# Five edits to an RWKV-then-soft-MoE kernel: queue of a small load, width and place of the v products, width of the second expert product, split of the last weight

## The chip, the cores and the metric

The kernel runs on one core of one Trainium2 chip. The metric is device time in microseconds, of the whole program. The kernel before takes 122.67 us, the median of 3 runs (122.54 to 122.88). The profile is one execution of the same program, with a span of 120.5 us (122.36 us by the metric).

## The reference

Two stages follow each other. The first is a linear attention with a decay for each channel (batch 4, 8 heads, 768 positions, head size 48); the second a soft mixture of experts (8 experts of 4 slots, model width 384, hidden width 1024) over all 3072 tokens.

```
for t in range(S):
    cur = einsum('bhd,bhe->bhde', u * k[t], v[t])
    y[t] = einsum('bhd,bhde->bhe', r[t], state + cur)
    state = w * state + einsum('bhd,bhe->bhde', k[t], v[t])
x = y as (B*S, H*D)
logits = x @ phi
d = softmax of logits over the tokens;   slot_input = d.T @ x
h = relu(slot_input[e] @ w1[e]);         slot_out[e] = h @ w2[e]
out = (softmax of logits over the slots) @ slot_out
```

## The kernel before, in words

**Units of work.** Two heads form a pair. A batch has 4 pairs, so there are 16 pairs, `nU`, numbered m or mu. A sequence of 768 is cut into 6 chunks of 128 positions, and these into two groups of three, `G = 2` and `L = 3`. A step i is one pair and one group: `mu, odd = divmod(i, 2)`, 32 steps in all, `nH`. The loop begins at i = -5, as the work is staged ahead: the step does the output of i, the state and mask of i + 1, and the preparation of the pair mu + 2.

**How the decay is taken in.** Instead of a loop over positions, k and r are scaled by powers of w: `W[0]` and `W[1]` are exp(position times ln w), built in the first steps by VectorE (line 188) and ScalarE (line 192). w itself comes to the core twice: `w_row`, one row which TensorE spreads over the partitions (`spread`, lines 177 and 178), and `wu`, from which `wu_steps` makes columns.

**The functions of a step.** `scale` multiplies raw k or r by W into kr (on GpSimd from the second pair on, line 228). `t_pe` transposes kr into the PSUM bank T0 (k, in even steps) or T1 (r, in odd steps), `t_evac` copies it to kT or rT on ScalarE (line 241). `b_pe` and `b_evac` turn kT back into kn, in order of position. `prod_f` multiplies kT by the transposed r. `v_cast` turns v to bf16 (line 270, ScalarE; GpSimd for the first pair). v lies in memory with three neighbouring positions in one partition; `v_pe` puts it in order of position with products by shifted parts of Q3 (line 284), into the bank Vb, and `v_evac` copies it to vn (line 290). `a_pe` multiplies kT by rT into Ab, `mask_f` masks it into AT (VectorE, line 304). `m_pe` builds the state of the chunks and the u term in Mb, `z_evac` makes Z and dv of it on VectorE (lines 341 and 342). `y_pe` adds up the output in Yb (lines 352, 363, 365), `y_evac` copies it to x (line 372, ScalarE).

**Routing.** From step 8 to step 31 `route` does the first part of the second stage for a batch that is done: transposes of x (`xt_mm`, then `xt_ev`, line 396, on ScalarE), logits, their exponential Le (line 402), the sums over tokens (`disp`, line 422) and the transposes of Le (`le_t`, `let_ev`). In `route`, s counts the eight steps of one batch; part 2 holds the ScalarE copies.

**Order.** Each instruction is recorded in the order in which the Python code calls it (`O(...)`), and each engine runs its own instructions in this order. The order of calls in a step, of those that the change touches or stands beside, is: `a_pe`, `mask_f`, `y_pe`, `y_evac`, `v_pe`, `v_evac`, `m_pe`, `z_evac`, `prod_f` or `b_pe`, `scale`, `route` part 0, `t_pe`, `route` part 1, `t_evac`, `v_cast`, `route` part 2, then exponentials of W and rows of zt where `T_AT` and `Z_AT` say so.

**Transfers.** SyncE issues k, r and v of the four batches in pieces (lines 115 and 119), each as soon as its place in three `raw` buffers is free. GpSimd issues the expert weights, w1 to w1_all and w2 into `raw` buffers that the batches have left (lines 135 and 138), at the steps in `W_AT`: the first at step 13, after a copy into `guard` that waits for the k of the last batch. The last weight, expert 7 of w2, is cut into three pieces along y.

**The end.** After the loop the experts run: a first product with w1 (line 623), its relu, transposes (line 648), and `second`, the product with w2 (line 660), which adds both groups of four experts into SO. Experts 6 and 7 come last, each as its weights land. SO is scaled into `so` in two halves, by VectorE (line 671) and ScalarE (line 672). Then 24 products of LexpT by so (line 684) are scaled and written out (lines 686, 688, 704).

The calls of a step that the change moves:

```
        if 0 <= i + 2 < nH:
            v_pe(i + 2)
            v_evac(i + 2)
...
        if odd == 0 and 0 <= mu + 2 < nU:
            v_cast(mu + 2)
        route(i, 2)
```

Of the kernel before, what the change touches and what calls it, by code (L numbers as in the profile page):

```python
# [9 lines left out]
def kernel(  # L10
# [13 lines left out]
    B, H, S, D = r.shape  # L24
    C = 128
    nC = S // C
    Nn, Dm = out.shape
    ES = moe_phi.shape[1]
    E = moe_w1.shape[0]
    F = moe_w1.shape[2]  # L30
    Spe = ES // E
    nM = Dm // C
    nF = F // C
    nQ = H // 2
    G = 2
    L = nC // G
    T = L * C
    P2 = 2 * D
    nN = Nn // C
    nG = B * G  # L40
    nU = B * nQ
    nH = nU * G
    J = S // C
    JV = T // C

    f32 = mybir.dt.float32
    bf = mybir.dt.bfloat16
    i32 = mybir.dt.int32
    AF = mybir.ActivationFunctionType
    ALU = mybir.AluOpType  # L50

    def O(ins):
        return tc.keep_in_program_order(ins)

    pe, dve, act, pool, sp = nc.tensor, nc.vector, nc.scalar, nc.gpsimd, nc.sync

    big = ctx.enter_context(tc.tile_pool(name="big", bufs=1))
    cst = ctx.enter_context(tc.tile_pool(name="cst", bufs=1))
    wk = ctx.enter_context(tc.tile_pool(name="wk", bufs=3))
# [5 lines left out]
    EG = E // 2  # L65
# [4 lines left out]
    def w2_of(e):  # L70
        g, j = divmod(e, EG)
        return raw[1 + g][:].bitcast(bf)[:, j * eW2:(j + 1) * eW2].rearrange("p (y d) -> p y d", y=nF)

    def raw_of(which, b):
        return raw[b % NR][:, which * RW:(which + 1) * RW]
# [5 lines left out]
    Yb = psb.tile([128, 512], f32, name="Yb")  # L81
    Xb = psb.tile([128, 512], f32, name="Xb")
    Vb = psb.tile([128, 512], f32, name="Vb")
# [11 lines left out]
    w_row = early[0:1, 0:H * D]  # L95
# [5 lines left out]
    phi_f = late[:, 128:128 + nM * ES]  # L101
    wu = cst.tile([8, 128], f32, name="wu")
    wu3 = wu[:].rearrange("q (e s) -> q e s", s=64)
    O(dve.memset(wu[:], 1.0))
    O(sp.dma_start(out=w_row, in_=w.rearrange("(o h) d -> o (h d)", o=1)))
    O(act.preload_act_table_set("natural_log_exp_and_others"))
    O(act.dma_start(out=wu3[0:4, :, 0:D], in_=w.rearrange("(q e) d -> q e d", e=2)))
    O(act.dma_start(out=wu3[4:8, :, 0:D], in_=u.rearrange("(q e) d -> q e d", e=2)))
# [44 lines left out]
    Q3 = cst.tile([128, QW], bf, name="Q3")  # L153
# [59 lines left out]
    ones = cst.tile([128, 128], bf, name="ones")  # L213
    Le_t = [cst.tile([128, L, 128], bf, name=f"Le{j}") for j in range(2)]
    phi_s = cst.tile([128, nM, ES], bf, name="phi_s")
    phi_b = cst.tile([128, nM * ES], bf, name="phi_b")
    assert JV == nM
    acc = cst.tile([128, NA], f32, name="acc")
    guard = cst.tile([128, 1], f32, name="guard")
    st = {}  # L220

# [51 lines left out]
    def at(i):  # L273
        m, g = divmod(i, G)
        b, q = divmod(m, nQ)
        return m, b, q, g, b * G + g

    def v_pe(i):
        m, b, q, g, n = at(i)
        vb = st["vb", m]  # L280
        for c in range(L):
            for j in range(JV):
                o = C * c - j + JV - 1
                O(pe.matmul(Vb[:, c * P2:(c + 1) * P2], Q3[:, o:o + C], vb[:, :, g, j, :],  # L284
                            start=(j == 0), stop=(j == JV - 1)))

    def v_evac(i):
        vn = wk.tile([128, L, 2, D], bf, name="vn", bufs=3)
        st["v", i] = vn
        O(act.copy(vn[:].rearrange("p c e d -> p (c e d)"), Vb[:, 0:L * P2]))  # L290

    def a_pe(i):
        m, b, q, g, n = at(i)
        kT, rT = st["kT", m], st["rT", m]
        for c in range(L):
            t = slice((g * L + c) * C, (g * L + c + 1) * C)
            for e in range(2):
                s = slice(64 * e, 64 * e + 64)
                O(pe.matmul(Ab[:, e, c * C:(c + 1) * C], kT[s, t], rT[s, t]))  # L299

    def mask_f(i):
        AT = wk.tile([128, 2, L, C], bf, name="AT", bufs=2)
        st["AT", i] = AT
        O(dve.tensor_mul(AT[:], Ab[:, :, 0:T].rearrange("p e (c t) -> p e c t", c=L),  # L304
                         mask_ut[:, None, None, :].to_broadcast([128, 2, L, C])))
# [99 lines left out]
    def le_t(n, lp=None):  # L405
        Le = st["Le", n]
        lp = le_p if lp is None else lp
        for c in range(L):
            O(pe.transpose(lp[:, c * C:(c + 1) * C], Le[:, c, :], ident[:]))
# [19 lines left out]
    def disp_ev(n, ds_p):  # L429
        if n == 0:  # L430
            O(dve.tensor_copy(acc[:], ds_p))
        else:
            O(dve.tensor_add(acc[:], acc[:], ds_p))
# [37 lines left out]
    Wf = [t[:].rearrange("p q j d -> p (q j d)") for t in W]  # L471
# [22 lines left out]
    for i in range(-5, nH):  # L494
        mu, odd = divmod(i, 2)
        if 0 <= i + 1 < nH:
            a_pe(i + 1)
            mask_f(i + 1)
        if pend:
            disp_ev(*pend.pop())  # L500
        if i == nH - 1:
            turn(n0, (2,), Vb[:].bitcast(bf), act)
            disp(n0 - 1, ds_t)
            le_t(n0 - 1)
            let_ev(n0 - 1, None, dve)
        if 0 <= i < nH:
            y_pe(i)
            y_evac(i)
        if 0 <= i + 2 < nH:
            v_pe(i + 2)  # L510
            v_evac(i + 2)
        if 0 <= i + 1 < nH:
            m_pe(i + 1)
            z_evac(i + 1)
        if odd == 0 and 0 <= mu + 1 < nU:
            prod_f(mu + 1)
        if odd and i > 0 and mu + 2 < nU:
            b_pe(mu + 2)
            b_evac(mu + 2)
        if odd and 0 <= mu + 3 < nU:  # L520
            scale(mu + 3, 0)
        if not odd and 0 <= mu + 2 < nU:
            scale(mu + 2, 1)
        route(i, 0)
        if 0 <= mu + 2 < nU:
            t_pe(mu + 2, odd)
            route(i, 1)
            t_evac(mu + 2, odd)
            if odd and i < 0:
                b_pe(mu + 2)  # L530
                b_evac(mu + 2)
        else:
            route(i, 1)
        if odd == 0 and 0 <= mu + 2 < nU:
            v_cast(mu + 2)
        route(i, 2)
        if i == nH - 3:
            turn(n0, (0, 1), T0, act)
        if i == nH - 2:
            turn(n1, (0, 1), T1, act)  # L540
        for f, j, q in T_AT.get(i, ()):
            f(j, q)
        if i in (-4, -3):
            wu_steps(i + 4)
        if i in Z_AT:
            q = Z_AT[i]
            O(act.activation(out=zt[:, q, 2, :], in_=zt[:, q, 0, :], func=AF.Copy, scale=wT[:, q:q + 1]))
        if i == 2:
            O(pool.memset(ones[:], 1.0))
            for t in Le_t:  # L550
                O(pool.memset(t[:], 0.0))
        if i == 3:
            load_kr(0, k, B - 1, 0, H)
            load_kr(1, r, B - 1, 0, H)
            for h0 in range(0, H, 2):
                load_v(B - 1, h0, h0 + 2)
        if i == 5:
            O(act.copy(phi_b[:], phi_f))
        if i == 6:
            for mi in range(nM):  # L560
                for j in range(nM):
                    o = C * mi - j + nM - 1
                    O(pe.matmul(Xb[:, mi * ES:(mi + 1) * ES].rearrange("p (j g s) -> p j g s", g=2, s=Spe),
                                Q3[:, o:o + C],
                                phi_b[:, j * ES:(j + 1) * ES].rearrange("p (g j s) -> p j g s", g=2, s=Spe),
                                start=(j == 0), stop=(j == nM - 1)))
            O(act.copy(phi_s[:].rearrange("p m s -> p (m s)"), Xb[:, 0:nM * ES]))
        if i == 28:
            O(pool.memset(uns, 0.0))
        if i == min(W_AT):  # L570
            O(pool.tensor_copy(guard[:], raw_of(0, B - 1)[:, 0:1]))
        for _ in range(W_AT.get(i, 0)):
            load_w(nw)
            nw += 1
    assert nw == 2 * E - 1
    for y0, y1 in ((0, 4), (4, 6), (6, 8)):
        load_w(nw, y0, y1)


# [29 lines left out]
    csr = cst.tile([128, 1], f32, name="csr")  # L609
# [8 lines left out]
    hT = [Wf[1].bitcast(bf)[:, g * F:(g + 1) * F].rearrange("p (y c) -> p y c", c=C) for g in range(2)]  # L618
    for g in range(2):
        for a in range(2):  # L620
            for mi in range(nM):
                for j in range(EG):
                    O(pe.matmul(hb[g][a][32 * j:32 * j + 32, 0:FH], uns[:, mi, g, j, :],
                                w1_all[:, g * EG + j, mi, a * FH:(a + 1) * FH],
                                start=(mi == 0), stop=(mi == nM - 1), skip_group_check=True))
            src = hb[g][a][:, 0:FH].rearrange("p (q y) -> p y q", y=nF)
            dst = h_sb[g][:, :, a * PH:(a + 1) * PH]
# [15 lines left out]
    HD = Dm // 2  # L643
# [7 lines left out]
        if g == 0:  # L651
            row_sums(0, 8)
    row_recip(0, 8)
    SO = [Xb[:, 0:HD], Yb[:, 0:HD]]

    def second(g, experts):
        for y in range(nF):
            for x in range(2):
                for j in experts:
                    O(pe.matmul(SO[x][32 * j:32 * j + 32, :], hT[g][:, y, 32 * j:32 * j + 32],  # L660
                                w2_of(g * EG + j)[:, y, x * HD:(x + 1) * HD],
                                start=(g == 0 and y == 0), stop=(g == 1 and y == nF - 1), skip_group_check=True))

    second(0, range(EG))
    second(1, range(EG - 2))
# [1 line left out]
    second(1, (EG - 2,))  # L667
    second(1, (EG - 1,))
    row_sums(8, 12)
    so = cst.tile([128, Dm], bf, name="so")  # L670
    O(dve.tensor_scalar_mul(so[:, 0:HD], SO[0], csr[:, 0:1]))
    O(act.activation(out=so[:, HD:Dm], in_=SO[1], func=AF.Copy, scale=csr[:, 0:1]))
    row_recip(8, 12)

    out_v = out.rearrange("(p n) m -> p n m", n=nN)
# [14 lines left out]
    i = 0  # L690
# [44 lines left out]
```

The softmax here doesn't subtract the row's maximum and nothing guards it: scores larger than these inputs give would overflow.

## Time and profile before

| what | value |
|---|---|
| time, median of 3 runs | 122.67 us (122.54 to 122.88) |
| span of the profile | 120.5 us, 4334 instructions |
| TensorE busy | 102.6 us, 85% |
| VectorE busy | 96.4 us, 80% |
| ScalarE busy | 83.7 us, 69% |
| GpSimd busy | 59.7 us, 50% |
| read from HBM, written | 39.38 MB, 4.72 MB |
| v products (line 284) | 288 of 128x96, 18.2 us busy |
| copies of v (line 290) | 32 of 128x288, mean 419 ns |
| casts of v (line 270) | 15 of 128x576, mean 677 ns |
| copies of kT, rT (line 241) | 32 of 128x768, mean 800 ns |

A busy time counts each instruction from its start to its end, and products overlap each other, so that 288 products of 211 ns take far less than their sum on the engine. How close they stand is read from the chain of waits or the timeline, which give when each group starts. A wait "A <- B" in the profile says that A's engine stood idle until B was done.

### The profile page before, as it was taken

What the parts mean: (1) busy time and instruction counts of PE and PEld (TensorE: products, weight loads), DVE (VectorE), ACT (ScalarE), POOL (GpSimd) and SP (SyncE); (2) the same over time, 40 slices, a digit from 0 to 9 for tenths busy, and PEclk for the clock granted to TensorE, in tenths of its full rate; (3) what the DMA queues carried; (4) which work ended last, traced back from release to release, by engine and by line L of the source; (5) the groups of instructions that cost most, each with busy time, mean ns of one, the idle gap of its engine ahead of it and who ended that gap; (6) DMA issues with size and microseconds to landing.
All of it is one profiled execution on the core that took longest, in us unless ns stands there. A gap on an engine that the chain in (4) does not pass through costs nothing.

```text
span 120.5 us, 4334 instructions
## 1 busy us (share of the span) xinstructions
PE 102.6 (85%) x1795; PEld 82.9 (69%) x1797; DVE 96.4 (80%) x187; ACT 83.7 (69%) x183; POOL 59.7 (50%) x70
## 2 busy tenths in 40 slices
PE   5996977799999999999999999999979996796000
PEld 1465866687887988898888898888866686583000
DVE  6899999999999999899999899999943510399000
ACT  4459769797978998888898988997963510299000
POOL 7349534599999999797677593101000000012000
PEclk9999999999999999999999999999999999999755
DMA  2999999999999999999999999999999998069992
GB/s 38 322 362 373 374 367 371 364 391 362 330 380 382 323 204 216 218 213 212 220 206 222 211 220 209 215 215 215 224 208 220 208 206 165 16 261 389 396 420 100
DMA packets 20925, 31.79 MB, mean 264 GB/s; under 512 B 1129, under 2 KB 18026, under 8 KB 20906
## 3 DMA queue, kind: packets, MB, share of 16 engines
q0 software_dynamic: 2960, 14.55, 55.5%
q1 hardware_dynamic: 17922, 16.96, 41.3%
q8 instruction: 14, 0.23, 0.7%
q14 instruction: 5, 0.04, 0.1%
q10 hardware_dynamic: 24, 0.00, 0.0%
HBM read 39.38 MB, written 4.72 MB: 366 GB/s over the span
## 4 chain that ended last, share of the span: by engine, by line
PE 37%; DMA 31%; DVE 15%; issue 6%; ACT 1%; POOL 1%; POOLq 0%; DVEq 0%; ACTq 0%
DMA raw<-in_moe_w_dram 31%; PE Vb L284 5%; PE T L235 4%; PE Ab L299 4%; PE Yb L352 3%; DVE W L188 3%; PE T L247 2%; PE Mb L325 2%; DVE prod L257 2%; PE Yb L365 2%; DVE kn L252 2%; DVE Z L341 2%; PE Xb L387 2%; PE Xb L380 2%; PE Yb L144 2%
## 5 line engine op out<-in xcount | busy, mean ns | idle before, releaser
L228 POOL TENSOR_TENSOR kr<-raw,W 128x576 bf16<-128x576 f32 x30 | 42.2, 1426 | 12.4 <-PE T L235 5.2
L304 DVE TENSOR_TENSOR AT<-Ab,mask_ut 128x768 bf16<-128x768 f32 x32 | 30.2, 945 | 0.8 <-PE Ab L299 0.6
L284 PE MATMUL Vb<-v_bf,Q 128*128 128x96 bf16 x288 | 18.2, 211 | 0.0
L235 PE MATMUL T<-ident,kr 128*128 128x128 bf16 x192 | 17.2, 230 | 1.0 <-POOL kr L228 1.0
L284 PEld LDWEIGHTS <-Q 128*128 128x128 bf16 x288 | 16.3, 100 | 1.5 <-issue 0.2
L241 ACT COPY kT<-T 128x768 bf16<-128x768 bf16 x16 | 12.8, 799 | 4.6 <-PE T L235 3.3
L241 ACT COPY rT<-T 128x768 bf16<-128x768 bf16 x16 | 12.8, 800 | 4.2 <-PE T L235 3.6
L257 DVE TENSOR_TENSOR prod<-T,kT 128x768 bf16<-128x768 bf16 x16 | 15.2, 947 | 0.0
L342 DVE TENSOR_TENSOR dv<-vn,Mb 128x288 bf16<-128x288 bf16 x32 | 14.1, 440 | 0.0
L235 PEld LDWEIGHTS <-kr 128*128 128x128 bf16 x192 | 12.7, 102 | 1.8 <-POOL kr L228 1.2
L290 ACT CAST vn<-Vb 128x288 bf16<-128x288 f32 x32 | 13.4, 419 | 0.1
L372 ACT CAST x<-Yb 128x288 bf16<-128x288 f32 x32 | 13.1, 409 | 0.2 <-PE Yb L365 0.2
L341 DVE TENSOR_TENSOR Z<-Mb,zt 128x288 bf16<-128x288 f32 (+1 forms) x32 | 12.7, 395 | 0.6
L299 PE MATMUL Ab<-rT,kT 64*128 64x128 bf16 x192 | 11.1, 222 | 2.1 <-DVE AT L304 2.1
L704 POOL DMA_DIRECT2D out_dram<-W x1 | 0.5, 549 | 24.9 <-DVE W L686 24.9
L325 PE MATMUL Mb<-vn,kn 128*128 128x96 bf16 (+2 forms) x80 | 11.5, 242 | 0.0
L352 PE MATMUL Yb<-vn,AT 128*128 128x48 bf16 x192 | 10.3, 185 | 0.1
L270 ACT CAST v_bf<-raw 128x576 bf16<-128x576 f32 x15 | 10.2, 677 | 0.0
L299 PEld LDWEIGHTS <-kT 64*128 64x128 bf16 x192 | 5.6, 95 | 5.6 <-DVE AT L304 2.0
L138 POOL DMA_DIRECT2D raw<-in_moe_w_dram x10 | 5.5, 557 | 7.9 <-DMA raw<-in_moe_w_dram 6.5
L352 PEld LDWEIGHTS <-AT 128*128 128x128 bf16 x192 | 7.1, 96 | 3.3
L365 PE MATMUL Yb<-dv,ident 128*128 128x288 bf16 x32 | 9.1, 285 | 0.2
(143 smaller groups left out, 221.7 us busy)
## 6 DMA issues: line engine op xcount, KB each, us to landing
w_all<-in_moe_w_dram POOLq DMA_DIRECT2D x8, 768.0 KB, 12.7
raw<-in_moe_w_dram POOLq DMA_DIRECT2D x7, 768.0 KB, 18.4
raw<-in_v_dram SPq DMA_DIRECT2D x12, 288.0 KB, 6.2
raw<-in_k_dram SPq DMA_DIRECT2D x8, 288.0 KB, 6.1
raw<-in_r_dram SPq DMA_DIRECT2D x8, 288.0 KB, 5.9
raw<-in_k_dram SPq DMA_DIRECT2D x2, 1152.0 KB, 12.9
raw<-in_r_dram SPq DMA_DIRECT2D x2, 1152.0 KB, 10.3
out_dram<-raw POOLq DMA_DIRECT2D x2, 768.0 KB, 6.8
```

Source lines behind the costliest of these rows:

```text
L228: O(eng.tensor_mul(kr[:, j].rearrange("p j (h s) -> p j h s", s=64)[:, :, :, 0:D], src, W[j][:, q].rearrange("p j (h d) -> p j h d", h=2)))
L235: O(pe.transpose(bank[:, x * C:(x + 1) * C], kr[:, j, x, :], ident[:]))
L241: O(act.copy(t[:].rearrange("p (s j) -> p s j", j=J), bank[:, 0:S].rearrange("p (j s) -> p s j", j=J)))
L257: O(dve.tensor_mul(pr[:].rearrange("p (s j) -> p s j", j=J), T1[:, 0:S].rearrange("p (j s) -> p s j", j=J), st["kT", m][:].rearrange("p (s ...
L284: O(pe.matmul(Vb[:, c * P2:(c + 1) * P2], Q3[:, o:o + C], vb[:, :, g, j, :], start=(j == 0), stop=(j == JV - 1)))
L290: O(act.copy(vn[:].rearrange("p c e d -> p (c e d)"), Vb[:, 0:L * P2]))
L299: O(pe.matmul(Ab[:, e, c * C:(c + 1) * C], kT[s, t], rT[s, t]))
L304: O(dve.tensor_mul(AT[:], Ab[:, :, 0:T].rearrange("p e (c t) -> p e c t", c=L), mask_ut[:, None, None, :].to_broadcast([128, 2, L, C])))
L325: O(pe.matmul(o, kn[:, g * L + c, :], vc, start=first, stop=True, skip_group_check=True))
L341: O(dve.tensor_mul(Z[:], Mb[:, 0:x * P2].rearrange("p (c e) -> p c e", c=x), zt[:, q, 0:x, :]))
L342: O(dve.tensor_mul(dv[:], st["v", i][:].rearrange("p c e d -> p (c e) d"), Mb[:, 288:288 + 2 * L, None].to_broadcast([128, L * 2, D])))
L352: O(pe.matmul(Yb[:, o:o + D], AT[:, e, c, :], vn[:, c, e, :], start=first, stop=False, skip_group_check=True))
```

## The change

- **w through ScalarE.** The load of `w_row` is issued by ScalarE instead of SyncE, so that the first k is the first transfer of SyncE.
- **v for a whole pair.** `v_pe` takes a pair, not a step: 9 products of 192 columns (both groups at once) instead of 9 of 96 columns in each step. Three chunks of 192 float columns do not fit in one bank, so the chunk c = 2 goes to the last 192 columns of Yb. `v_evac` has two copies, and `vn` is one buffer for the pair. Both run in even steps, for the pair mu + 1; `v_cast` moves from the even to the odd step.
- **w2 in 384 columns.** `second` writes the whole width of 384 at once into Xb, instead of two halves of 192 in Xb and Yb. Both halves of `so` are then read from Xb.
- **The last piece of one row.** The last weight is cut at y = 4 and y = 7 instead of 4 and 6.
- **Places.** `phi_b` lies in the buffer of `acc`, and `so` in W[1]; this makes room for the wider `vn`.

```diff
-    O(sp.dma_start(out=w_row, in_=w.rearrange("(o h) d -> o (h d)", o=1)))
+    O(act.dma_start(out=w_row, in_=w.rearrange("(o h) d -> o (h d)", o=1)))
...
-    phi_b = cst.tile([128, nM * ES], bf, name="phi_b")
+    phi_b = acc[:].bitcast(bf)[:, 0:nM * ES]
...
-    def v_pe(i):
-        m, b, q, g, n = at(i)
+    VW = G * P2
+
+    def v_pe(m):
         vb = st["vb", m]
         for c in range(L):
+            dst = Vb[:, c * VW:(c + 1) * VW] if c < 2 else Yb[:, 512 - VW:512]
             for j in range(JV):
                 o = C * c - j + JV - 1
-                O(pe.matmul(Vb[:, c * P2:(c + 1) * P2], Q3[:, o:o + C], vb[:, :, g, j, :],
-                            start=(j == 0), stop=(j == JV - 1)))
-
-    def v_evac(i):
-        vn = wk.tile([128, L, 2, D], bf, name="vn", bufs=3)
-        st["v", i] = vn
-        O(act.copy(vn[:].rearrange("p c e d -> p (c e d)"), Vb[:, 0:L * P2]))
+                O(pe.matmul(dst.rearrange("p (g e d) -> p g e d", g=G, e=2), Q3[:, o:o + C],
+                            vb[:, :, :, j, :].rearrange("p e g d -> p g e d"),
+                            start=(j == 0), stop=(j == JV - 1), skip_group_check=True))
+
+    def v_evac(m):
+        vn = wk.tile([128, G, L, 2, D], bf, name="vn", bufs=2)
+        for g in range(G):
+            st["v", m * G + g] = vn[:, g]
+        O(act.copy(vn[:, :, 0:2].rearrange("p g c e d -> p g c (e d)"),
+                   Vb[:, 0:2 * VW].rearrange("p (c g x) -> p g c x", c=2, g=G)))
+        O(act.copy(vn[:, :, 2].rearrange("p g e d -> p g (e d)"),
+                   Yb[:, 512 - VW:512].rearrange("p (g x) -> p g x", g=G)))
...
-        if 0 <= i + 2 < nH:
-            v_pe(i + 2)
-            v_evac(i + 2)
+        if odd == 0 and 0 <= mu + 1 < nU:
+            v_pe(mu + 1)
+            v_evac(mu + 1)
...
-        if odd == 0 and 0 <= mu + 2 < nU:
+        if odd and 0 <= mu + 2 < nU:
             v_cast(mu + 2)
...
-    for y0, y1 in ((0, 4), (4, 6), (6, 8)):
+    for y0, y1 in ((0, 4), (4, 7), (7, 8)):
...
-    SO = [Xb[:, 0:HD], Yb[:, 0:HD]]
+    SO = Xb[:, 0:Dm]
...
-            for x in range(2):
-                for j in experts:
-                    O(pe.matmul(SO[x][32 * j:32 * j + 32, :], hT[g][:, y, 32 * j:32 * j + 32],
-                                w2_of(g * EG + j)[:, y, x * HD:(x + 1) * HD],
-                                start=(g == 0 and y == 0), stop=(g == 1 and y == nF - 1), skip_group_check=True))
+            for j in experts:
+                O(pe.matmul(SO[32 * j:32 * j + 32, :], hT[g][:, y, 32 * j:32 * j + 32],
+                            w2_of(g * EG + j)[:, y, :],
+                            start=(g == 0 and y == 0), stop=(g == 1 and y == nF - 1), skip_group_check=True))
...
-    so = cst.tile([128, Dm], bf, name="so")
-    O(dve.tensor_scalar_mul(so[:, 0:HD], SO[0], csr[:, 0:1]))
-    O(act.activation(out=so[:, HD:Dm], in_=SO[1], func=AF.Copy, scale=csr[:, 0:1]))
+    so = Wf[1].bitcast(bf)[:, 2 * F + nM * ES * 8:2 * F + nM * ES * 8 + Dm]
+    O(dve.tensor_scalar_mul(so[:, 0:HD], SO[:, 0:HD], csr[:, 0:1]))
+    O(act.activation(out=so[:, HD:Dm], in_=SO[:, HD:Dm], func=AF.Copy, scale=csr[:, 0:1]))
```

More of the change, by code (lines that the diff above doesn't have):

```diff
@@ L557 @@
         if i == 5:
-            O(act.copy(phi_b[:], phi_f))
+            O(act.copy(phi_b, phi_f))
         if i == 6:
```

## The prediction

> **What bounds the kernel now.** I read the page's slices first, then the waits at the end, then the timeline around the last weights, and last the main loop, engine by engine.
>
> ```profile
> PE   5996977799999999999999999999979996796000
> ...
> DVE  6899999999999999899999899999943510399000
> ACT  4459769797978998888898988997963510299000
> ...
> DMA  2999999999999999999999999999999998069992
> ```
>
> A slice is 3.01 us. The DMA row is full from slice 1 to slice 32: k, r, v first (GB/s near 370), then the weights (near 213), with no hole. So the last weight lands when the stream of bytes is through. The list of waits agrees: "PE Xb L660 <- DMA" is 1.9 us in 4 waits, and the chain of waits gives the weights 31% of the span. The timeline shows how close the compute is behind:
>
> ```profile
> 99.43 1.42 PEld L660 LDWEIGHTS <-W 128*32 128x32 bf16 x17 [0.23 <-issue]
> 99.60 0.24 PE L660 MATMUL Xb<-raw,W 128*32 128x192 bf16 x1 [0.42 <-DMA raw<-in_moe_w_dram]
> ...
> 101.94 0.24 PE L660 MATMUL Xb<-raw,W 128*32 128x192 bf16 x1 [0.86 <-DMA raw<-in_moe_w_dram]
> ...
> 103.83 0.24 PE L660 MATMUL Xb<-raw,W 128*32 128x192 bf16 x1 [0.41 <-DMA raw<-in_moe_w_dram]
> ...
> 104.28 0.42 DVE L671 TENSOR_SCALAR so<-Xb,csr 128x192 bf16<-128x192 f32 x1 [7.27 <-PE Xb L660]
> 104.36 0.42 ACT L672 ACTIVATE so<-Yb,csr 128x192 bf16<-128x192 f32 x1 [7.53 <-PE Yb L660]
> ```
>
> Without any DMA wait, expert 6 could start near 99.35 (its weight load stood ready at 99.43) and needs 16 products at 0.083 us, 1.33 us; expert 7 the same: done at 102.0 instead of 104.16. So the compute has 2.1 us of slack. A main loop later by more than that sets the end itself.
>
> The main loop (14 to 88 us) has no slack of its own. Here is the chain, from the end of an odd step's transposes of r (L235) into the next, even step:
>
> ```profile
> 57.63 0.33 PE T L235 x6
> 57.96 0.28 PE Ab L299 x6
> 58.24 0.25 PE Yb L352 x6
> 58.70 0.38 PE Vb L284 x9
> 59.17 0.12 PE Mb L325 x2
> ```
>
> and ScalarE in the same stretch:
>
> ```profile
> 58.00 0.80 ACT L241 COPY rT<-T 128x768 bf16<-128x768 bf16 x1 [0.24 <-PE T L235]
> 58.70 0.49 ACT L396 COPY xT<-Xb 128x384 bf16<-128x384 bf16 x1
> 59.07 0.42 ACT L372 CAST x<-Yb 128x288 bf16<-128x288 f32 x1
> 59.36 0.43 ACT L290 CAST vn<-Vb 128x288 bf16<-128x288 f32 x1
> 60.03 0.80 ACT L241 COPY kT<-T 128x768 bf16<-128x768 bf16 x1 [0.24 <-PE T L235]
> 60.72 0.68 ACT L270 CAST v_bf<-raw 128x576 bf16<-128x576 f32 x1
> ```
>
> The reader is to see three things. TensorE runs gap-free, one pair of steps taking 58.70 to 63.32, 4.62 us (its busy time in 44 to 64 us is 19.82 of 20.00). ScalarE starts the copy of rT 0.04 us after the transposes, always after an idle 0.24: it is not behind, it waits for TensorE. And the cast of v (L270) stands in the even step, after kT: its result is read by v_pe two steps later.
>
> **What the Trainium skill says.** "PSUM — Partial Sum Buffer", section "PSUM bank collisions raise a hardware error": PSUM is to be guarded by bank, not by address, ScalarE against VectorE too. In the trace of before the two copies of so (104.28, 104.36) overlap, and they read two banks; no run yet shows two readers of one. The same page, "Engine vs sequencer instructions": ScalarE's queue is strict FIFO; the rows above fit. "TensorE: Matmul & The Clock Gate", "Back-to-back issue gap": N/2.4 + 2.5 ns when warm, 42.5 ns for 96 columns and 82.5 for 192. The trace has 0.38/9 = 42 ns for 96, so 82 for 192 is taken. "DMA: Bandwidth & Descriptors", "Issuing engines are not separate DMA queues": issuing elsewhere saves only issue time. In the trace w's issue stands at 0.74 and k's at 1.14.
>
> **The change, part by part.**
>
> *w through ScalarE.* k's issue moves from 1.14 to 0.74, the full stream starts 0.40 us sooner: -0.40 on the landing of the last weight, if that still ends last. ScalarE's table load (1.28 us) starts some 0.35 us later, hidden before L178 at 3.91; w and u for wu land as much later, hidden before L203 at 7.70.
>
> *v in wide products.* TensorE: 18 products of 96 columns (0.76 us a pair) become 9 of 192 (0.74): nothing. ScalarE: two copies of 288 (0.42 each) become one of 384 and one of 192. From 288 at 0.40 and 768 at 0.80 the slope is 0.83 ns an element, so 0.48 + 0.32: nothing. What counts is where they stand. In the changed order of instructions:
> - v_cast moves to the odd step, behind the copy of rT. v_pe, in the next step, waits for it. Between the last transpose of r and v_pe TensorE has 12 instructions of a_pe and 18 of y_pe.
> - The third product, c = 2, goes to Yb, and waits (bank guard) for the copy x<-Yb of the same step, which on ScalarE stands behind rT, v_cast and xT.
>
> Walk from the start of the rT copy, with the pitches above: v_cast starts at 0.70 and ends at 1.38; v_pe starts at 1.44 (0.06 for the semaphore, as between xT's end at 48.16 and the load at 48.22) instead of 0.70. Six products: to 1.94. ScalarE: xT at 0.70 + 0.57 = 1.27, x at 1.64, done 2.06; so the three into Yb run from 2.12 to 2.37, and m_pe starts at 2.37 instead of 1.17 (59.17 less 58.00). That is +1.20; the odd step saves its 0.38: **+0.82 us a pair**. Where the exponential Le stands between (0.14), 0.98. With the transposes of Le (every fourth pair) about 0.70. Where no xT is there yet (steps 4 to 8), v_cast alone binds, m_pe at 2.19: +0.64. Queued behind the stalled v_pe on TensorE are m_pe, the routing products, the transposes; VectorE waits for all of these with Z, dv, prod. Nothing hides it, as TensorE has no gap.
>
> Sum over even steps: 10 to 28: 5 x 0.82 + 3 x 0.98 + 2 x 0.70 = 8.4. Steps 4, 6, 8: 3 x 0.6 = 1.8. Steps 0 and 2: the copy x of these steps stands behind the exponential of W (L192) and zt (17.09 and 22.93 in before), so the c = 2 product, and m_pe, come some 1.2 and 1.1 later than VectorE wants: 2.3. Start: v_cast(0) on GpSimd moves from the idle spot at 7.34 behind the scaling of k that starts at 9.27 (1.4 each), so it runs 10.65 to 11.86, and v_pe(0) starts at 11.95 instead of 9.28; TensorE's row had some 1 us of idle there, and the first mask moves from 13.39 to about 14.8: 1.4. Sum 8.4 + 1.8 + 2.3 + 1.4 = **13.9 us** for the main loop.
>
> The early steps are least sure: from 0.5 to 5 instead of 3.7. The pair: from 0.6 (VectorE, at 4.42 us a pair in 24 to 42 us, was already holding TensorE a little) to 1.0.
>
> *Weights.* GpSimd issues the first weight at step 13, at 40.22 before. With 7 us of delay by then it is issued at about 47.5, while k, r, v are through at about 43: the DMA row gets a hole of 6 us, and the last weight lands at about 110. The compute without waits ends at 102.0 + 13.9 = 115.9, so this hides beside it.
>
> *w2 of 384 columns.* 64 products of 0.165 for 128 of 0.083: nothing. But both halves of so now read one bank, and in the changed order ScalarE's waits for VectorE's: 0.42 + 0.06 later, where before it was 0.08 later. TensorE's second output product waits for it, and all outputs stand behind: +0.4, less 0.1 for a last group of one product instead of four: +0.3 on the tail.
>
> *Last piece of one row.* It would save some 0.2 us where the last landing sets the end; the weights will have landed: nothing. *phi_b in acc, so in W:* other places, no wait on the path: nothing.
>
> Sum: 13.9 - 2.1 (slack) + 0.3 = +12.1 us, 134.8; I take **134.5**, as a little of the early delay will overlap.
>
> **Rivals.**
> - The transfers still set the end and the stalls vanish in the 2.1 us slack: -0.4 + 0.3 - 0.1, 122.5, no change or just faster. For it: the DMA row is full. Against it: 15 pairs would have to stall under 0.14 us each, and v_cast alone (0.68) starts after rT.
> - The stalls are partly taken up by waits for VectorE hidden inside the chain's pieces, 0.4 a pair; the hole in the weights then sets the end together with the compute: weights at 108 to 110, +4 to +6, 127 to 129.
> - The stalls are larger, since kT's copy and b_pe also slip and the granted clock falls in the gaps (as the PEclk row does, to 7 and 5, once TensorE idles at the end): 1.2 a pair, 18 + 3 - 2: 140.
>
> **How the numbers follow.** Main case 0.76, from 129.5 to 138.5; partial stall 0.13; no stall 0.07; larger 0.04. The pair's bounds give 15 x 0.6 + 0.5 - 1.8 = 7.7 and 15 x 1.0 + 5 - 1.8 = 18, not both at once: range 129 to 139. Only the no-stall case can be faster or equal: faster 0.04, same 0.03, slower 0.93.
>
> **What would show it.** Right: TensorE idle 0.6 to 0.9 us before v_pe in every even step, released by ScalarE's v_bf, and again before the products into Yb by x; VectorE's share in 44 to 84 us falls from 97% to about 82%; first weight issued after 46 us and a hole in the DMA row near 43 to 48; no DMA wait left before expert 7; the two copies of so one after the other. Wrong: pairs still at 4.6 us, or the last L660-like products still waiting for a weight.

## The result, and the profile after

The changed kernel took **137.98 us** (136.71 to 138.43), the kernel before 122.62 us beside it: ratio 1.122, 95% interval 1.117 to 1.127. It is slower by 15.4 us; the prediction was 134.5 us in a range of 129 to 139.

From the page of the changed kernel, the same rows as before, with slices of 3.4 us instead of 3.0:

```profile
PE   6976966679889797877979787797978899989000
...
DVE  6996769697797696959669695966969344079300
ACT  3566676775877767686776768678677544069200
...
DMA  4999999999992599999999999999999900019993
```

The DMA row has the predicted hole, in slices 12 and 13, and ends at slice 31 (some 109 us), well before the outputs. TensorE and VectorE now have gaps in a regular beat through the whole loop. The windows view puts numbers on it, for 44 to 84 us (columns: stretch, its length, busy time and instructions of PE, PEld, DVE, ACT, POOL, granted clock, DMA share, GB/s):

```profile
44.00:84.00 40.00, 33.13 (x580) 26.91 (x579) 30.49 (x57) 29.23 (x65) 25.49 (x28) 1.00 0.97 191
```

VectorE is busy 30.49 of 40 us, 76%, where it was 38.74, 97%. The list of waits (us in total, times, longest us) names what TensorE stood for:

```profile
DVE Z L348 <- PE Mb L336: 16.9, 15, 1.6
...
PE Vb L286 <- ACT v_bf L270: 8.7, 14, 0.7
...
PEld L336 <- DVE prod L257: 4.2, 12, 0.5
...
PE Yb L286 <- ACT x L379: 2.7, 5, 1.2
```

None of the four is in the list of the kernel before. The first is VectorE waiting for the sums that TensorE delivers late. The second is the predicted wait for the cast of v, once in nearly every pair. The third was not predicted. The fourth is the predicted wait of the third product for the copy x.

The chain of waits through one pair (start, us, what) shows the second and the third in one line of descent:

```profile
68.70 0.80 ACT rT L241
69.50 0.58 ACT v_bf L270
70.08 0.04 issue
70.12 0.66 PE Vb L286 x6
70.78 0.03 issue
70.80 0.41 PE Yb L286 x3
71.21 0.08 PE Mb L321
...
71.78 0.45 DVE dv L349
72.23 0.88 DVE prod L257
73.11 0.05 issue
73.15 0.23 PE Mb L336 x3
...
74.35 0.80 ACT rT L241
```

Before, TensorE's own work made this chain, and a pair took 4.62 us. Now the chain goes from engine to engine: copy of rT and cast of v on ScalarE, products of v and sums into Mb on TensorE, then Z, dv and prod on VectorE, and the second sums (73.15) of the pair wait for prod. A pair takes 74.35 - 68.70 = 5.65 us. And ScalarE beside it:

```profile
68.70 0.80 ACT L241 COPY rT<-T 128x768 bf16<-128x768 bf16 x1 [0.84 <-DVE Z L348]
69.39 0.68 ACT L270 CAST v_bf<-raw 128x576 bf16<-128x576 f32 x1
69.97 0.48 ACT L403 COPY xT<-Xb 128x384 bf16<-128x384 bf16 x1
70.34 0.41 ACT L379 CAST x<-Yb 128x288 bf16<-128x288 f32 x1
```

The copy x, which frees Yb for the third product, ends at 70.75; the products into Yb start at 70.80.

At the end, the last products with w2 run without a break, and the two copies of so follow one another (timeline of the changed kernel):

```profile
114.34 2.78 PE L666 MATMUL Xb<-raw,W 128*32 128x384 bf16 x48
...
117.37 2.14 PE L666 MATMUL Xb<-raw,W 128*32 128x384 bf16 x16
...
119.55 0.42 DVE L677 TENSOR_SCALAR W<-Xb,csr 128x192 bf16<-128x192 f32 x1 [4.56 <-PE Xb L666]
...
120.00 0.42 ACT L678 ACTIVATE W<-Xb,csr 128x192 bf16<-128x192 f32 x1 [5.20 <-DVE W L677]
```

Where the 15.7 us between the two spans (136.2 and 120.5) went is a sum of three readings. The last copy of Z in the loop (tile 31) starts at 105.38 instead of 87.39, +18.0. From there to the first copy of so it takes 14.17 us instead of 16.89, -2.7. The first output leaves 1.65 us after that copy's start instead of 1.28, +0.4. Below, "loop delay" is the first of these: the start of that last copy of Z against the kernel before. It can be read for each of the 32 copies of Z; "tile n" is the copy number n, counted from 0, and step i makes tile i + 1. In the profiles of runs 1, 3, 6 and 9, and in one of run 8 (w's queue with the last piece), the granted clock averages only 0.83 to 0.91 over 10 to 30 us (1.00 in the others), and what that costs is in their loop delays; from 30 to 88 us it is 1.00 in all.

### The profile page after: what moved, and what is told of

The parts are those of the page before. It is cut to its first block, busy times and chain, and to the rows that moved or that the text cites. A ratio compares the mean times of both kernels' runs of the same rounds, so it can differ in the third digit from the quotient of the medians.

```text
span 136.2 us, 3901 instructions
## 1 busy us (share of the span) xinstructions
PE 105.8 (78%) x1589; PEld 80.1 (59%) x1589; DVE 96.1 (71%) x187; ACT 85.3 (63%) x183; POOL 58.6 (43%) x70
## 4 chain that ended last, share of the span: by engine, by line
PE 30%; DMA 22%; DVE 17%; ACT 11%; issue 8%; POOL 3%; SPq 1%; POOLq 0%; DVEq 0%
DMA raw<-in_moe_w_dram 16%; DVE prod L257 7%; DMA raw<-in_v_dram 7%; PE Vb L286 4%; ACT v_bf L270 4%; DVE dv L349 4%; PE Xb L666 4%; PE T L247 3%; PE Yb L286 3%; ACT rT L241 3%; PE T L235 3%; POOL raw L138 2%; PE Mb L336 2%; DVE W L188 2%; PE Mb L332 1%
## 5 line engine op out<-in xcount | busy, mean ns | idle before, releaser
L228 POOL TENSOR_TENSOR kr<-raw,W 128x576 bf16<-128x576 f32 x30 | 41.7, 1402 | 29.7 <-PE T L235 15.8
L348 DVE TENSOR_TENSOR Z<-Mb,zt 128x288 bf16<-128x288 f32 (+1 forms) x32 | 12.9, 403 | 16.9 <-PE Mb L336 16.9
L286 PEld LDWEIGHTS <-Q 128*128 128x128 bf16 x144 | 13.0, 100 | 18.8 <-issue 18.1
L286 PE MATMUL Vb<-v_bf,Q 128*128 128x192 bf16 x96 | 10.9, 252 | 10.7 <-ACT v_bf L270 8.7
L235 PEld LDWEIGHTS <-kr 128*128 128x128 bf16 x192 | 12.9, 103 | 0.6 <-DVE kr L228 0.5
L379 ACT CAST x<-Yb 128x288 bf16<-128x288 f32 x32 | 13.1, 409 | 0.1
L359 PE MATMUL Yb<-vn,AT 128*128 128x48 bf16 x192 | 10.4, 186 | 0.0
L270 ACT CAST v_bf<-raw 128x576 bf16<-128x576 f32 x15 | 10.1, 675 | 0.0
L294 ACT CAST vn<-Vb 128x384 bf16<-128x384 f32 x16 | 7.7, 478 | 3.0 <-PE Vb L286 2.3
L247 PE MATMUL T<-ident,kT 128*128 128x128 bf16 x96 | 8.6, 230 | 1.1 <-DVE acc L440 0.6
L252 DVE COPY kn<-T 128x768 bf16<-128x768 bf16 x16 | 8.8, 552 | 0.3 <-PE T L247 0.3
L286 PE MATMUL Yb<-v_bf,Q 128*128 128x192 bf16 x48 | 6.8, 251 | 2.9 <-ACT x L379 2.7
```

Source lines behind the costliest of these rows:

```text
L228: O(eng.tensor_mul(kr[:, j].rearrange("p j (h s) -> p j h s", s=64)[:, :, :, 0:D], src, W[j][:, q].rearrange("p j (h d) -> p j h d", h=2)))
L235: O(pe.transpose(bank[:, x * C:(x + 1) * C], kr[:, j, x, :], ident[:]))
L247: O(pe.transpose(T0[:, c * C:(c + 1) * C], kT[:, c * C:(c + 1) * C], ident[:]))
L270: O(act.copy(out, src))
L286: O(pe.matmul(dst.rearrange("p (g e d) -> p g e d", g=G, e=2), Q3[:, o:o + C], vb[:, :, :, j, :].rearrange("p e g d -> p g e d"), start=(j ...
L348: O(dve.tensor_mul(Z[:], Mb[:, 0:x * P2].rearrange("p (c e) -> p c e", c=x), zt[:, q, 0:x, :]))
```

## The experiments

Two theories stand behind the expectations. **P**: the loss comes from places in ScalarE's in-order queue, the cast behind the copy of rT first of all, and the copy x that the third product waits for. **V**: the loss is made in the odd step, where the second sums into Mb wait for VectorE's product of k and r, which is late because Z is. Later ones refine or oppose P, and say so.

**1. The cast back in the even step**, all else as changed.

```diff
-        if odd and 0 <= mu + 2 < nU:
+        if odd == 0 and 0 <= mu + 2 < nU:
             v_cast(mu + 2)
```

> The changed kernel with the cast of v back in the even step; all else stays, the third product still goes to Yb. Theory P (place in the queue: v_pe waits for a cast that stands behind the copy of rT, and the product into Yb waits for the copy x behind it): the wait for v_bf before v_pe vanishes, the wait for x shrinks to about 0.3 us where xT stands before it and to nothing where it doesn't; steps 0 and 2 still wait for x behind the exponential. Some 8 us less than the changed kernel: 129 to 131 us. Rival W (the width: products of 192 and copies of 384 and 192 cost more than they save): no difference, 137 to 138.

Measured: 131.75 us (131.65 to 132.42), ratio 1.077 (1.073 to 1.081); loop delay 11.8 instead of 18.0. The wait for v_bf is gone from the list of waits, and these are left:

```profile
DVE Z L348 <- PE Mb L336: 11.6, 15, 1.2
...
PEld L336 <- DVE prod L257: 5.4, 13, 1.3
PE Yb L286 <- ACT x L379: 5.3, 10, 1.7
```

So the cast's place is worth 6.2 us of the 15.4, a little less than expected. The expectation was wrong on the third product's wait for x: it did not shrink, it grew from 2.7 us in 5 waits to 5.3 us in 10.

**2. The product of k and r earlier**: `prod_f` called right behind `mask_f`, before the copies of Z; the cast stays in the odd step.

```diff
             mask_f(i + 1)
+        if odd == 0 and 0 <= mu + 1 < nU:
+            prod_f(mu + 1)
...
             z_evac(i + 1)
-        if odd == 0 and 0 <= mu + 1 < nU:
-            prod_f(mu + 1)
```

> The changed kernel with prod_f moved ahead of z_evac in the even step, into the hole of 1.0 to 1.5 us in which VectorE waits for m_pe. Theory V (a second gate: with no v_pe in the odd step, m_pe comes 0.38 us sooner, but its last products wait for prod, so that the saving is not had): the wait of L336 for prod vanishes and each pair is 0.3 to 0.4 us shorter, 13 pairs: 132.5 to 134. Rival (the saving was lost elsewhere, prod waits only because all is late): 137 to 138.

Measured: 131.99 us (131.75 to 132.82), ratio 1.079 (1.074 to 1.084); loop delay 12.9. The wait of L336 for prod is gone, and that for the cast is as it was (9.4 us in 14 waits). The gain is larger than expected. V is no rival to P then: it is a second gate in the same pair, worth 6.0 us in time, about as much as the cast.

**3. The cast alone in the odd step, on the kernel before**: the narrow products of v stay, one set a step, all into Vb.

```diff
-        if odd == 0 and 0 <= mu + 2 < nU:
+        if odd and 0 <= mu + 2 < nU:
             v_cast(mu + 2)
```

> The kernel before with one edit: the cast of v in the odd step. Products of 96 columns in each step, no use of Yb. Theory P with the cast as the larger part: v_pe waits 0.7 us in every even step, and no saving stands against it: 0.7 x 14 plus about 1 us at the start, less 2.7 of slack: 130 to 132. If the wait for x (Yb) were the larger part: 123 to 126.

Measured: 129.04 us (128.63 to 129.33), ratio 1.053 (1.050 to 1.057); loop delay 8.7, and the list of waits has "PE Vb L284 <- ACT v_bf L270" at 9.2 us in 14. One condition changed, no work added: 6.5 us. It is a little under the expectation and near the 6.2 us that run 1 gained by the reverse edit.

**4. The order of v late in the even step**, behind `t_evac`, so that it no longer comes before the sums; the cast stays in the odd step.

```diff
-        if odd == 0 and 0 <= mu + 1 < nU:
-            v_pe(mu + 1)
-            v_evac(mu + 1)
...
             t_evac(mu + 2, odd)
...
+        if odd == 0 and 0 <= mu + 1 < nU:
+            v_pe(mu + 1)
+            v_evac(mu + 1)
         if odd and 0 <= mu + 2 < nU:
             v_cast(mu + 2)
```

> The changed kernel with v_pe and v_evac called at the end of the even step, after t_evac; the cast stays in the odd step, the products stay wide and the third goes to Yb. Theory P: by then the cast and the copy x are long done, v_pe waits for nothing, pairs return to 4.4 to 4.8 us, and the transfers set the end again: 122 to 124 us. Rival W (the width): no less than 130. Rival: m_pe of the odd step now waits for the copies of v: 125 to 128.

Measured: 133.77 us (133.05 to 133.98), ratio 1.093 (1.089 to 1.097): a clear miss. The loop delay tells why: counted from tile to tile it stays between -0.7 and +0.2 us up to tile 8, so until then neither the wide products nor their place cost anything, and grows to 13.1 from tile 12 on, with the routing. There (timeline, ScalarE first, TensorE after it):

```profile
63.77 0.80 ACT L241 COPY rT<-T 128x768 bf16<-128x768 bf16 x1 [0.84 <-PE T L235]
64.47 0.68 ACT L270 CAST v_bf<-raw 128x576 bf16<-128x576 f32 x1
65.04 0.48 ACT L403 COPY xT<-Xb 128x384 bf16<-128x384 bf16 x1
...
65.58 0.24 PE L387 MATMUL Xb<-phi_s,xT 128*128 128x32 bf16 x3 [0.84 <-ACT xT L403]
...
67.82 0.31 PE L359 MATMUL Yb<-vn,AT 128*128 128x48 bf16 x6 [0.47 <-ACT vn L296]
```

The cast no longer holds back its own consumer, but it stands ahead of xT, and the products for the logits (L387) wait for that instead; TensorE is idle 0.84 us at 65.58. The theory has to be wider than its first form: in the odd step every result that comes behind the cast in ScalarE's queue is late. The last line is a second loss, with no cast in it: the third product of v now stands in Yb when the next output sums (L359) want the bank, and they wait until ScalarE has copied it out, 6.6 us in 15 waits. How the 13.1 us divide between the two was not tested.

**5. The order of v behind the sums, the cast in the even step.** Against run 1 this moves only v's place.

```diff
-        if odd == 0 and 0 <= mu + 1 < nU:
-            v_pe(mu + 1)
-            v_evac(mu + 1)
         if 0 <= i + 1 < nH:
             m_pe(i + 1)
             z_evac(i + 1)
         if odd == 0 and 0 <= mu + 1 < nU:
+            v_pe(mu + 1)
+            v_evac(mu + 1)
             prod_f(mu + 1)
```

> The changed kernel with two moves: the cast of v back in the even step, and v_pe and v_evac called after m_pe and z_evac of the even step (m_pe of that step uses the pair before). Wide products, third product in Yb, all other edits stay. If only places in the queues cost: by the time TensorE reaches v_pe the cast has long been done, and x is copied by the time of the third product (1.04 + 0.50 after the start of rT, against x at 1.48), so pairs return to 4.4 to 4.7 us and the transfers set the end: 122.2 to 123.2 us. If wide products or copies cost by themselves, or prod still gates m_pe: over 125.

Measured: 125.24 us (124.73 to 126.22), ratio 1.022 (1.017 to 1.026); loop delay 4.8. It is 6.5 us better than run 1, and still 2 more than expected. Up to tile 11 the delay is 0.4, and then it grows again with the routing. In the even step xT stands behind the two copies of v, kT and the cast (timeline of ScalarE):

```profile
57.07 0.48 ACT L294 CAST vn<-Vb 128x384 bf16<-128x384 f32 x1 [0.28 <-PE Vb L286]
57.45 0.32 ACT L296 CAST vn<-Yb 128x192 bf16<-128x192 f32 x1
57.79 0.80 ACT L241 COPY kT<-T 128x768 bf16<-128x768 bf16 x1
58.49 0.68 ACT L270 CAST v_bf<-raw 128x576 bf16<-128x576 f32 x1
59.06 0.48 ACT L403 COPY xT<-Xb 128x384 bf16<-128x384 bf16 x1
```

and TensorE's products for the logits start at 59.60, after 0.41 us of idle time.

**6. Both gates away, the order of v still ahead of the sums**: runs 1 and 2 together.

> The changed kernel with both waits of the odd and even step's v order taken away: the cast of v back in the even step, and the product of k and r called right after the mask, ahead of the copies of Z. The order of v for a pair stays ahead of the sums into Mb, with its third product in Yb. Theory P (two separate gates: the cast's place cost 6.1 us of the loop, the late product 5.1 us, and they add): loop delay against the kernel before of 18.0 - 6.1 - 5.1 = 6.8 us, less some 2.7 us of slack in the transfers plus 0.4 us at the end, time 125.5 to 127.5 us; the waits of L336 for prod and of Vb for v_bf are gone, and what is left is the wait of the third product for the copy x out of Yb, over 4 us. Rival S (both gates hide behind the same third wait, for x, so taking away the second one brings little): 129.5 to 131.5 us.

Measured: 129.14 us (128.43 to 129.97), ratio 1.053 (1.046 to 1.060). The gains of runs 1 and 2 do not add: 8.8 us together, 6.2 and 6.0 alone. The same holds in the loop delay of steps 10 to 28 by itself, where the clock is 1.00: 4.5 us together, 3.6 and 2.4 alone. The time lies between the two expectations, and meets neither. The waits that are left are x before the third product, 5.6 us in 10, as in run 1, and the weight loads of the logits waiting for xT, 3.7 us in 8 where run 1 had 1.9 in 6. So part of what one edit freed was taken by the next gate of the same queue.

**7. The cast behind xT**, on run 5.

```diff
+        route(i, 2)
         if odd == 0 and 0 <= mu + 2 < nU:
             v_cast(mu + 2)
-        route(i, 2)
```

> The order of v for a pair called after the sums into Mb in the even step, as in the run that took 125.2 us, with the cast of v in the same step but behind the copies of the routing (ScalarE: kT, xT, cast in place of kT, cast, xT). Theory Q (what was left there were the logits' waits for xT, 3.7 us in 8, behind the two copies of v and the cast; whatever stands behind the cast and has a consumer soon pays for it): the waits of L387 for xT drop under 1.5 us, loop delay 2 to 3 us in place of 4.8, the transfers set the end again, 122.4 to 123.4 us. Rival C (ScalarE is by then full in the even step, and the cast behind xT only hands its 0.7 us on to the copy x of the odd step): xT's waits go, those of Yb for x or of the products behind it grow, 124.7 to 125.7 us.

Measured: 122.59 us (122.14 to 123.59), ratio 1.0005 (0.998 to 1.003): the time of the kernel before, as theory Q had it; loop delay 1.1, and no wait of the logits for xT. ScalarE in the same stretch:

```profile
56.58 0.80 ACT L241 COPY kT<-T 128x768 bf16<-128x768 bf16 x1
57.28 0.48 ACT L403 COPY xT<-Xb 128x384 bf16<-128x384 bf16 x1
57.65 0.69 ACT L270 CAST v_bf<-raw 128x576 bf16<-128x576 f32 x1
58.22 0.41 ACT L379 CAST x<-Yb 128x288 bf16<-128x288 f32 x1
```

The same instructions as in the changed kernel, in another order, take 15.4 us less. A pair from the copy of rT at 58.61 to the next at 63.19 takes 4.58 us, as before the change. The last weights set the end again: TensorE waits 0.87 us for one at 103.18.

**8. The change without its part on v**: w through ScalarE, last piece of one row, w2 in 384 columns, on the kernel before.

> The kernel before with every edit of the change but those on v: w through ScalarE's queue, last piece of one row, w2 in products of 384 columns into one bank. Theory P (the loop's order of v is all of the loss; the other edits are worth +0.4 and -0.2 us, as measured alone): 122.6 to 123.2 us, no wait for v_bf, x or prod that the kernel before has not. Rival R (the small edits only hurt beside each other, through the order in which the transfers start): over 124 us.

Measured: 122.85 us (122.55 to 123.70), ratio 1.0024 (1.0009 to 1.0039). Two parts of it were run alone. **w2 in 384 columns:**

> The kernel before with one edit: the second product of the experts in 384 columns into Xb. Theory: the copy of so by ScalarE waits for that by VectorE (0.42 + 0.03), instead of starting 0.08 after it; less 0.1 for the shorter last group: 0.25 to 0.4 us slower, 122.8 to 122.95. Rival: hidden, or the wide product saves more: 122.3 to 122.6.

Measured: 123.09 us, ratio 1.0031 (1.0013 to 1.0048): +0.4 us, as expected. **w through ScalarE with the last piece of one row:**

> The kernel before with two edits: the load of w_row through ScalarE, and the last weight cut at 4 and 7. Theory: the transfers start 0.40 us sooner and, being without a hole, end as much sooner; the last piece of one row saves up to 0.2 us: 121.9 to 122.2. Rival: the start of the transfers isn't what the last landing depends on, no difference: 122.5.

Measured: 122.50 us, ratio 0.9984 (0.9967 to 1.0002): less than expected, and not told apart from nothing. The profile of the three edits together shows where the earlier start went: k is issued at 0.74 instead of 1.14, but GpSimd issues the first weight when it comes to step 13, at 40.26 against 40.22, and the first of the late weights lets expert 6 start at 99.70 against 99.60. All three together cost 0.3 us (0.1 to 0.5).

**9. w2 in halves again, on runs 5 and 7.** On run 5:

> The same with the second product of the experts as in the kernel before (two halves of 192 columns in two banks). If the transfers set the end, the 0.40 us of the earlier first k is had, and the output phase loses nothing: 121.9 to 122.3 us, 0.3 to 0.4 us less than the run with 384 columns, and faster than both kernels. If the loop is still behind: as the run with 384 columns.

On run 7:

> The same with w2 in two products of 192 columns into two banks, as in the kernel before, so that the two copies of the output do not share a bank. If the end is set by the transfers (theory Q): 0.3 to 0.5 us less than the same with 384 columns, 122.0 to 123.0 us. If the loop still sets it (theory C): up to 1 us more than the same with 384 columns, since the wide products of the last weights overlap.

Measured: 126.69 us (125.73 to 127.06), ratio 1.031 (1.027 to 1.035), and 123.75 us (123.66 to 123.92), ratio 1.009 (1.007 to 1.011). Both are over 1 us slower than the same with 384 columns, and both expectations missed. Most of the loss is not where the edit is. On run 5, from the last copy of Z to the first of so takes 14.49 us with halves and 14.16 without, and the first output then leaves after 1.28 us instead of 1.65: together nothing. But in both pairs of profiles the loop of the kernel with halves falls behind early; in the second pair (run 7 and this one) the delay of Z is 1.8 us at tile 4, against 0.4. The windows of TensorE show it. First run 7:

```profile
22.00:24.00 2.00, 0.34 (x5) 0.34 (x5) 2.00 (x5) 1.61 (x4) 0.86 (x1) 1.00 1.10 382
24.00:26.00 2.00, 2.00 (x41) 1.74 (x39) 1.99 (x4) 1.88 (x5) 2.00 (x5) 1.00 1.08 390
```

then the same with w2 in halves:

```profile
22.00:24.00 2.00, 0.27 (x4) 0.15 (x2) 2.00 (x5) 1.44 (x4) 0.68 (x1) 0.98 1.09 370
24.00:26.00 2.00, 2.00 (x25) 1.59 (x24) 1.33 (x3) 1.37 (x4) 2.00 (x5) 0.50 1.09 391
```

In both, TensorE has stood for 1.7 us at step 2 (third product, waiting for x behind the exponential of W); in the second the granted clock is then 0.50, and 25 products are done in 2 us instead of 41. Seen in windows of 1 us, the clock of the second is 0.50 from 24 to 27 us, and had been 0.50 from 14 to 17 us too; in run 7's profile it is 1.00 over both stretches. Why the kernels with halves met this more often is open. Nor is the clock all of it: the one execution with halves on run 5 that has a mean clock of 0.975 took 125.73 us, where the three without halves at 0.978 took 124.73 to 124.75. So no gain from halves is seen, and the cause of the loss stays open.

## Why the prediction was right, and where it was off

**The gate of the cast**: right. It was placed at 1.44 us after the start of the rT copy, with the products into Yb at 2.12 and the first sums at 2.37. The profile after has 1.42 and 2.10 (68.70, 70.12 and 70.80 above), and 2.35 for the first sums, whose own start the timeline gives (the chain counts each piece from the end of the one ahead):

```profile
71.05 0.24 PE L321 MATMUL Mb<-Z,ident 128*128 128x192 bf16 x1
```

From tile to tile, the even steps 10 to 28 added 1.23 us each to the loop delay; the prediction's sum has 1.22 on average, its 1.20 with the corrections for Le. That the two agree so closely is in part luck. The 1.17 from which the 1.20 was counted is the second group of sums (L325); the first (L314) starts at 58.92 in the timeline of before, 0.92 after rT. So the first sums come 1.43 later after rT, and 0.18 of this is made up because rT now starts 0.48 us after the copy of Z ahead of it instead of 0.66.

Runs 1 and 3 show the cause by undoing it and by doing it alone. The Trainium skill's sentence that ScalarE's queue is strict FIFO (PSUM — Partial Sum Buffer, "Engine vs sequencer instructions") fits: 6.5 us in run 3 from one place in such a queue.

**The term that was mis-sized: the 0.82 us a pair.** It was 1.20 of delay in the even step, less 0.38, since "the odd step saves its 0.38" of v's products. That saving is the step that failed: the odd steps 10 to 28 gave back 0.04 us each instead of 0.38, and so the pairs of these steps cost 11.9 us in 10, 1.2 a pair, in place of 8.4. The odd step's second sums do come up sooner on TensorE, but they wait for prod, which VectorE makes after Z and dv, and these are late by the even step's delay. Run 2 shows it: with prod early the wait of L336 goes, and the odd steps 10 to 28 give back 0.59 us each. Its even steps cost more, 1.54 instead of 1.23, for a reason that no run isolates, so that a pair costs 0.96. Of the 5.1 us of loop delay that run 2 saves, 2.4 fall in these steps and 2.7 before them. The dependence stood in the profile of before (prod on VectorE, then the products of L329, there without a wait), but the walk followed TensorE and ScalarE through the odd step and left VectorE out. The rival "1.2 a pair" had the right number for other reasons: the granted clock is 1.00 over 44 to 84 us, so no clock was behind it, and the copy of kT, its other reason, is not in the chain of that pair.

**The other terms.** The start cost 0.8 us instead of 1.4, as the cast on GpSimd took 0.66 us (from 10.68) and not 1.21; steps 0 and 2 cost 2.8 instead of 2.3; steps 4 to 8, 2.4 instead of 1.8. The slack was 2.7, not 2.1: the products of the last two experts write different column tiles and, as the timeline has them, overlap a little: 16 of them in the 2.07 us from 117.37 to 119.44, where 16 x 0.165 makes 2.6. In halves and without a wait for weights (run 3) the slack is 2.4, so that 0.3 of it comes with the wide products. The tail cost 0.4, predicted 0.3: the copies of so stand one after the other on one bank, as the Trainium skill asks (PSUM — Partial Sum Buffer, "PSUM bank collisions raise a hardware error": guard PSUM by bank, not by address), and run 8's part on w2 alone costs the same 0.4. These misses go both ways and nearly cancel. What is left of the 3.5 us by which 134.5 was too low is the pair.

**The hole in the weights**: right in kind, 3 us early: the first weight is issued at 44.24 instead of 47.5, as GpSimd is only 4.0 us behind the kernel before there, and the last lands near 109 instead of 110. No product of L666 waits for one. Two of the signs named in advance were missed in size: the first weight was to be issued after 46, and VectorE's share to fall to about 82%, where it fell to 76%.

**The 0.4 us of w's queue** could not be seen in the changed kernel, as predicted. The step itself does not hold on the kernel before either: it had the earlier start arrive at the last weight because the transfers have no hole, but the weights begin when GpSimd reaches step 13, and that did not move (run 8). w's queue and the last piece together gave -0.2 us, within the measurement's uncertainty.

**What the whole loss is made of**, by runs that each differ from the one before in one place: 137.98 as changed; 131.75 with the cast in the even step; 125.24 with v ordered behind the sums; 122.59 with the cast behind xT. All 15.4 us come back by moving calls alone, with every other edit of the change in place, so they are places in queues. The wide products of v stay in run 7, whose loop is 1.1 us late in the profile; the slack before the last weights hides that, and the time is that of the kernel before within 0.4 us. So they gain nothing that can be seen. No version beat the kernel before beyond what these runs can tell.

## What to carry to other kernels

Before an operation is moved in an in-order queue, list not only its own consumer but every result that then comes behind it, on that engine, and how soon each is wanted; when one gate is taken away, look for the next one in the same queue. A stall of one engine is paid again by the engines that wait for it, so walk a delay through all engines once around the loop before a saving elsewhere is set against it. Where a merged operation must stand somewhere, put it behind the results that the critical engine wants next.

## What the runs showed that was not expected

Of the twelve executions of run 7, the six with a mean granted clock of 0.973 or more took 122.14 to 122.63 us; of the six at 0.947 to 0.961, five took 123.25 to 123.59. The profiles of run 9 show such a fall, to 0.50 for some 3 us from 24 us on, after TensorE had stood for 1.7 us. It costs 1.3 us there (the delay goes from 0.5 at tile 3 to 1.8 at tile 4). But an idle time of this length does not decide it alone: run 7 and run 5 have the same gap (1.73 and 1.74 us, ending at 23.66), with the clock at 1.00 behind it. What else it takes is not shown.

Wide and narrow products of v are worth the same to TensorE: six of 192 columns start in 0.49 us in run 4 (66.17 to 66.66), 82 ns each, twice the 42 ns that 96 columns took before.
